# Moving two of the first four loads to ScalarE's queue in a fused retention and GELU kernel

## The chip, the cores and the metric

The kernel runs on one core of one Trainium2 chip. The metric is the device time of one execution in microseconds (us). Every ratio, with its 95% interval, is taken between the runs of two kernels of the same rounds; it is not quite the ratio of the medians that are quoted beside it. A difference counts as faster or slower from 2% on.

## The reference

Retention attention (8 batches, 8 heads, 576 positions, head size 64) feeds a two-layer network with a tanh GELU:

```python
scores = scale * np.matmul(q, k.transpose(0, 1, 3, 2))
gamma = 1.0 - 2.0 ** (-5.0 - np.arange(H, dtype=np.float32))
Dmat = np.where(rel >= 0, gamma[:, None, None] ** rel[None, :, :], 0.0)
ret = np.matmul(scores * Dmat[None], v)
# ... ret -> x, 4608 tokens x 512
h = x @ w_in                                    # 512 x 2048
g = 0.5 * h * (1.0 + np.tanh(c * (h + 0.044715 * h * h * h)))
out = g @ w_out                                 # 2048 x 512
```

## The kernel before

Work is laid out by hand in a plan of small steps. The plan fixes each engine's order. Only the start of the kernel ("the head", until the first long run of up-projection matmuls, called hp) matters for the main part of the change. Five pieces take part in it.

ScalarE's order begins with the decay factors. The trace shows a table load of 1.28 us in front of the first exp (at 0.73 us) and a second one, also of 1.28 us, in front of a dummy Gelu (at 3.99 us); the rest of the execution has none:

```python
nc.scalar.activation(out=p2[:, 3:4], in_=wz[:, 0:1], func=AF.Exp)      # first table load
# ...
for p in range(HP):
    nc.scalar.activation(out=gx[:, p], in_=gi, func=AF.Exp, bias=lg[:, 12:13], scale=lg[:, 8 + p : 9 + p])
nc.scalar.activation(out=sc, in_=ex, func=AF.Exp, bias=0.0, scale=-1.0)
gt = const.tile([128, HP], F32, name="gt")
nc.scalar.activation(out=gt, in_=lg[:, 8:12], func=AF.Exp, bias=0.0, scale=128.0)
nc.scalar.activation(out=p2[:, 3:4], in_=wz[:, 0:1], func=AF.Gelu_apprx_tanh)   # second table load
```

SP issues all loads of the head, each of 256 KB, in this order:

```python
load_qkv(0, 0, 0, "k", None)
load_qkv(0, 0, 0, "q", None)
load_qkv(0, 0, 1, "k", None)
load_qkv(0, 0, 0, "v", None)
load_qkv(0, 0, 1, "q", None)
# ... in load_qkv: nc.sync.dma_start(out=t..., in_=SRC[key][b, ...])
```

GpSimd (POOL) clears a buffer, then casts q and k. TensorE transposes the two cast tiles. The copies out of PSUM belong to ScalarE (the whole first tile and half of the second) and VectorE (the other half):

```python
(0, L(tbd_zero, 0, G)),
(0, L(cast_qk, 0, 0, 0, "q", G)),
(0, L(cast_qk, 0, 0, 0, "k", G)),
(0, L(mask)),
(0, L(tr, 0, 0, 0, 1, A)),      # ScalarE copies
(0, L(cast_v, 0, 0, 0, G)),
(0, L(tr, 0, 0, 0, 0, S2)),     # S2: half ScalarE, half VectorE
(0, L(score_mm, 0, 0, 0)),
```

Finally, `pads` puts a fixed number of dummy 128-column matmuls ("pads") in front of a step, for example `("tr", 0, 0, 1, 0): 24`.

## Time and profile before

| | before |
|---|---|
| time, median of the first 3 runs | 298.46 us (298.14 to 299.01) |
| span of the profiled run | 296.3 us |
| first copy on ScalarE starts | 5.78 us |
| VectorE's half copy starts | 6.80 us |
| first long hp run starts | 22.46 us |

The page's first part gives busy time, share of the span and instruction count of each engine. Its third part gives the DMA queues (packets, MB, share of the 16 DMA engines' time). Queue q1 is the one that SP feeds, q10 the one that ScalarE feeds (before the change, with stores at the end of the kernel only):

```profile
PE 288.9 (97%) x3748; PEld 208.6 (70%) x3748; DVE 230.7 (78%) x434; ACT 162.0 (55%) x316; POOL 122.4 (41%) x142
...
q1 hardware_dynamic: 94336, 51.26, 67.7%
q10 hardware_dynamic: 336, 0.66, 0.8%
```

TensorE is the bound, and ScalarE's average of 55% says nothing of the head, where it is full until 5.48 us. Two entries of TensorE's timeline (start, duration, engine, line, operation) serve as marks: the second group of score matmuls, and the long hp run.

```profile
10.41 0.42 PE L395 MATMUL st<-T 64*64 64x128 f16 x16
22.46 2.78 PE L669 MATMUL hp<-x,w_in_sb 128*128 128x256 f16 x24 [0.92 <-DVE x L535]
```

### The profile page before, as it was taken

What the parts mean: (1) busy time and instruction counts of PE and PEld (TensorE: products, weight loads), DVE (VectorE), ACT (ScalarE), POOL (GpSimd) and SP (SyncE); (2) the same over time, 40 slices, a digit from 0 to 9 for tenths busy, and PEclk for the clock granted to TensorE, in tenths of its full rate; (3) what the DMA queues carried; (4) which work ended last, traced back from release to release, by engine and by line L of the source; (5) the groups of instructions that cost most, each with busy time, mean ns of one, the idle gap of its engine ahead of it and who ended that gap; (6) DMA issues with size and microseconds to landing.
All of it is one profiled execution on the core that took longest, in us unless ns stands there. A gap on an engine that the chain in (4) does not pass through costs nothing.

```text
span 296.3 us, 8910 instructions
## 1 busy us (share of the span) xinstructions
PE 288.9 (97%) x3748; PEld 208.6 (70%) x3748; DVE 230.7 (78%) x434; ACT 162.0 (55%) x316; POOL 122.4 (41%) x142
## 2 busy tenths in 40 slices
PE   8989999999999999999999999999999999999995
PEld 6866578888884568656875587558755886786584
DVE  2795899999997795898569856877688198886753
ACT  7329789865546762665446544555345217605720
POOL 6734774476240144086026305469003005711760
PEclk9999999999999999999999999999999999999999
DMA  7999999868779999994998899482120003002204
GB/s 201 308 354 326 315 383 323 222 177 210 166 239 182 291 274 173 283 291 104 194 295 243 124 209 306 146 146 18 60 86 0 2 22 124 0 2 71 71 3 142
DMA packets 94712, 52.48 MB, mean 177 GB/s; under 512 B 38352, under 2 KB 88528, under 8 KB 94672
## 3 DMA queue, kind: packets, MB, share of 16 engines
q1 hardware_dynamic: 94336, 51.26, 67.7%
q10 hardware_dynamic: 336, 0.66, 0.8%
q8 instruction: 29, 0.48, 0.7%
q14 instruction: 11, 0.09, 0.1%
HBM read 36.70 MB, written 9.44 MB: 156 GB/s over the span
## 4 chain that ended last, share of the span: by engine, by line
PE 78%; DVE 13%; DMA 4%; ACT 2%; issue 1%; SPq 0%; POOL 0%; DVEq 0%; ACTq 0%
PE hp L583 31%; PE my L726 9%; PE mz L726 9%; PE mw L726 5%; PE mu L726 4%; PE mv L726 4%; PE hp L669 3%; DMA T<-kq 3%; DVE ret L408 3%; PE st L395 2%; PE xs L495 2%; PE py L613 2%; DVE ost L753 2%; PE xs L522 2%; DVE x L535 1%
## 5 line engine op out<-in xcount | busy, mean ns | idle before, releaser
L583 PE MATMUL hp<-x,w_in_sb 128*128 128x512 f16 x408 | 94.0, 379 | 0.0
L587 ACT ACTIVATE gT<-hp 128x512 f16<-128x512 f32 x112 | 65.8, 598 | 41.9 <-PE hp L583 40.1
L583 PEld LDWEIGHTS <-w_in_sb 128*128 128x128 f16 x448 | 42.5, 98 | 44.5 <-issue 0.3
L726 PEld LDWEIGHTS <-gT 128*128 128x128 f16 x576 | 55.8, 98 | 8.0
L232 POOL CAST kq<-ld 128x512 f16<-128x512 f32 x31 | 22.0, 716 | 57.7 <-DMA ld<-in_k_dram 42.3
L241 POOL TENSOR_TENSOR cv<-ld,sc 128x512 f16<-128x512 f32 x28 | 32.8, 1184 | 28.4 <-DMA ld<-in_v_dram 23.8
L408 DVE TENSOR_TENSOR ret<-st,cm 128x512 f16<-128x512 f32 x64 | 40.0, 681 | 4.2 <-PE st L395 3.9
L232 ACT CAST tbd<-ws 64x256 f16<-64x256 f32 x61 | 24.6, 403 | 22.5 <-DVE ws L476 21.9
L726 PE MATMUL my<-w_out_sb,gT 128*128 128x256 f16 x288 | 34.4, 273 | 0.0
L726 PE MATMUL mz<-w_out_sb,gT 128*128 128x256 f16 x288 | 34.4, 273 | 0.0
L726 PEld LDWEIGHTS <-gsum 128*128 128x128 f16 x288 | 28.0, 98 | 3.4
L698 DVE TENSOR_TENSOR gT<-gT 128x1024 f16<-128x1024 f16 x30 | 28.6, 960 | 0.2
L694 DVE TENSOR_TENSOR gsum<-gT 128x1024 f16<-128x1024 f16 x32 | 25.7, 802 | 2.7 <-ACT gT L656 2.7
L535 DVE TENSOR_TENSOR x<-xs,gx 128x512 f16<-128x512 f32 x32 | 21.5, 683 | 4.8 <-PE xs L522 4.6
L753 DVE TENSOR_TENSOR ost<-ost,mv 128x512 f32<-128x512 f32 x18 | 11.5, 683 | 16.6 <-issue 11.7
L686 DVE TENSOR_TENSOR gdia<-gT 128x512 f16<-128x512 f16 (+1 forms) x30 | 21.9, 731 | 2.8 <-ACT gT L587 2.1
L694 POOL TENSOR_TENSOR gsum<-gT 128x1024 f16<-128x1024 f16 x4 | 8.9, 2222 | 34.8 <-ACT gT L656 31.8
L669 PE MATMUL hp<-x,w_in_sb 128*128 128x256 f16 x160 | 19.0, 273 | 1.0 <-DVE x L535 0.9
L669 PEld LDWEIGHTS <-w_in_sb 128*128 128x128 f16 x160 | 15.3, 98 | 3.1 <-issue 1.3
L726 PE MATMUL mu<-w_out_sb,gsum 128*128 128x256 f16 x144 | 17.2, 273 | 0.1
L726 PE MATMUL mw<-w_out_sb,gdia 128*128 128x256 f16 x144 | 17.2, 273 | 0.0
L726 PE MATMUL mv<-w_out_sb,gsum 128*128 128x256 f16 x144 | 17.2, 273 | 0.0
(114 smaller groups left out, 402.2 us busy)
## 6 DMA issues: line engine op xcount, KB each, us to landing
ld<-in_k_dram SPq DMA_DIRECT2D x30, 256.0 KB, 5.3
ld<-in_q_dram SPq DMA_DIRECT2D x30, 256.0 KB, 5.4
ld<-in_v_dram SPq DMA_DIRECT2D x30, 256.0 KB, 5.7
out_dram<-ost SPq DMA_DIRECT2D x14, 512.0 KB, 5.2
loan<-in_moe_w_out_dram SPq DMA_DIRECT2D x12, 256.0 KB, 5.4
loan<-in_moe_w_in_dram SPq DMA_DIRECT2D x8, 256.0 KB, 5.8
ld<-in_moe_w_in_dram SPq DMA_DIRECT2D x8, 256.0 KB, 6.0
ld<-in_moe_w_out_dram SPq DMA_DIRECT2D x4, 256.0 KB, 5.6
```

The lines of the kernel that those rows point to most:

```text
L232: (eng.copy if eng is nc.scalar else eng.tensor_copy)(out=out, in_=in_)
L241: eng.tensor_tensor(out=unperm(att[b]["v"][:, s, hh, :]), in0=perm(t), in1=sc[:, 8 * hh : 8 * hh + 8] .rearrange("p (r h) -> p r h", r=2) ...
L408: nc.vector.tensor_tensor(out=x.rearrange("p (a m) -> p a m", a=2), in0=st[hl].rearrange("p (a m) -> p a m", a=2), in1=cm.rearrange("p r s ...
L535: nc.vector.tensor_tensor(out=xb[b][:, :, 2 * s + c].rearrange("p s q i -> p q s i"), in0=att[b]["x", s][c].rearrange("p (q s i) -> p q s ...
L583: nc.tensor.matmul(hp, w_in_sb[:, ct, 128 * f : 128 * f + 128], x[:, :, ct, :], start=(ct == 0), stop=(ct == 3),)
L587: nc.scalar.activation(out=self.g(f // 2)[:, f % 2], in_=hp, func=AF.Gelu_apprx_tanh)
L669: nc.tensor.matmul(hp[:, 256 * h : 256 * h + 256], w_in_sb[:, ct, 256 * j + 128 * h : 256 * j + 128 * h + 128], xb[self.b][:, :, 2 * u : 2 ...
L686: e.tensor_tensor(out=self.sa[:, j : j + n], in0=g[:, :, 0, 0:256], in1=g[:, :, 1, 256:512], op=ALU.add)
L694: e.tensor_tensor(out=self.sc[:, j : j + n], in0=g[:, :, 0], in1=g[:, :, 1], op=ALU.add)
L698: e.tensor_tensor(out=g.rearrange("p j h c -> p j (h c)")[:, :, 256:768].rearrange("p j (h c) -> p j h c", h=2), in0=g[:, :, :, 0:256], in ...
L726: nc.tensor.matmul(o, lhs(j, slice(128 * u, 128 * u + 128)), w_out_sb[:, j, w], start=((u == 0 or isinstance(t, list)) and j == 0 and not ...
L753: nc.vector.tensor_tensor(out=out, in0=in0, in1=t, op=op)
```

## The change

The intent is to get q, which the first cast waits for, and v sooner, by issuing them from a second queue at the same moment as SP issues k. ScalarE's exps move behind these two issues. The core of the diff:

```diff
-    nc.scalar.activation(out=p2[:, 3:4], in_=wz[:, 0:1], func=AF.Exp)
...
+    def exps():
+        nc.scalar.activation(out=p2[:, 3:4], in_=wz[:, 0:1], func=AF.Exp)
+        for p in range(HP):
+            nc.scalar.activation(out=gx[:, p], in_=gi, func=AF.Exp, ...)
+        ...                                    # sc, gt, dummy Gelu, as before
...
-            nc.sync.dma_start(
+            (nc.scalar if (b, key, s, hh) in AQ else nc.sync).dma_start(
...
+    AQ = {(0, "q", 0, 0), (0, "v", 0, 0)}
...
     load_qkv(0, 0, 0, "v", None)
+    exps()
     load_qkv(0, 0, 1, "q", None)
```

The rest of the diff touches the end of the kernel. The product called my runs its j loop outside. In the units with three PSUM banks, two subtractions of 256 columns become one of 512, ScalarE copies the first bank straight into the tile that they work on, and the two halves of that bank change places. Some helpers for half-sized state steps are defined but not called:

```diff
-            for m, k in ((2, 0), (1, 1)):
-                nc.vector.tensor_tensor(out=q4[:, m], in0=pw[:, 0:256], in1=c2[:, k], op=ALU.subtract)
+            nc.vector.tensor_tensor(
+                out=q[:, 1:3],
+                in0=pw[:, 0:256].unsqueeze(1).to_broadcast([128, 2, 256]),
+                in1=q[:, 1:3],
+                op=ALU.subtract,
+            )
...
+            order = [(u, j) for j in js for u in us] if m == "my" else [(u, j) for u in us for j in js]
```

More of the change, by code (lines that the diff above doesn't have):

```diff
@@ L119 @@
     gx = const.tile([128, HP, 2, 64], F32, name="gx")
-    for p in range(HP):
-        nc.scalar.activation(out=gx[:, p], in_=gi, func=AF.Exp, bias=lg[:, 12:13], scale=lg[:, 8 + p : 9 + p])
-    nc.scalar.activation(out=sc, in_=ex, func=AF.Exp, bias=0.0, scale=-1.0)
     gt = const.tile([128, HP], F32, name="gt")
-    nc.scalar.activation(out=gt, in_=lg[:, 8:12], func=AF.Exp, bias=0.0, scale=128.0)
-    nc.scalar.activation(out=p2[:, 3:4], in_=wz[:, 0:1], func=AF.Gelu_apprx_tanh)
+    def exps():
+        nc.scalar.activation(out=p2[:, 3:4], in_=wz[:, 0:1], func=AF.Exp)
+        for p in range(HP):
+            nc.scalar.activation(out=gx[:, p], in_=gi, func=AF.Exp, bias=lg[:, 12:13], scale=lg[:, 8 + p : 9 + p])
+        nc.scalar.activation(out=sc, in_=ex, func=AF.Exp, bias=0.0, scale=-1.0)
+        nc.scalar.activation(out=gt, in_=lg[:, 8:12], func=AF.Exp, bias=0.0, scale=128.0)
+        nc.scalar.activation(out=p2[:, 3:4], in_=wz[:, 0:1], func=AF.Gelu_apprx_tanh)
     tbd = [const.tile([128, NC, HP, 128], F16, name=f"tbd{i}") for i in range(2)]
@@ L442, in mask_tail, with state_h, state_mm @@
             a["rett", hl] = x
-    def state_mm(b, ss):
+    def state_h(b, s, hh):
+        state_mm(b, [s], (hh,))
+    def state_mm(b, ss, hhs=(0, 1)):
         a = att[b]
         us = [bank("us") for _ in range(2)]
-        pad(("us", b, ss[0]), us[0])
+        pad(("us", b, ss[0]) if len(hhs) == 2 else ("us", b, ss[0], hhs[0]), us[0])
         for n, s in enumerate(ss):
-            a["U", s] = us, n
-            for p in range(HP):
+            for hh in hhs:
+                a["U", s, hh] = us, n
+            for p in range(2 * hhs[0], 2 * hhs[-1] + 2):
                 hh, pp = divmod(p, 2)
@@ L464, in state_mm, with scan, scan_h, put @@
                             )
-    def scan(b, n):
+    def scan(b, n, hhs=(0, 1)):
         a = att[b]
         s, c = divmod(n, 2)
-        us, i = a["U", s]
-        uc = us[c][:, 256 * i : 256 * i + 256].rearrange("p (q d) -> p q d", d=64)
+        us, i = a["U", s, hhs[0]]
+        qs = slice(2 * hhs[0], 2 * hhs[-1] + 2)
+        nq = qs.stop - qs.start
+        uc = us[c][:, 256 * i : 256 * i + 256].rearrange("p (q d) -> p q d", d=64)[:, qs]
         if n > 0:
-            t = sb.tile([128, HP, 64], F32, tag="vs", name="vs", bufs=1)
-            nc.vector.tensor_tensor(out=t, in0=uc, in1=a["w", n - 1], op=ALU.add)
+            t = sb.tile([128, HP, 64], F32, tag="vs", name="vs", bufs=1)[:, qs]
+            nc.vector.tensor_tensor(out=t, in0=uc, in1=a["w", n - 1][:, qs], op=ALU.add)
             uc = t
-        w = sb.tile([128, HP, 64], F32, tag="ws", name="ws", bufs=2)
-        nc.vector.tensor_tensor(out=w, in0=uc, in1=gt.unsqueeze(2).to_broadcast([128, HP, 64]), op=ALU.mult)
-        a["w", n] = w
-    def put(b, n, eng):
+        if ("w", n) not in a:
+            a["w", n] = sb.tile([128, HP, 64], F32, tag="ws", name="ws", bufs=2)
+        nc.vector.tensor_tensor(
+            out=a["w", n][:, qs], in0=uc, in1=gt[:, qs].unsqueeze(2).to_broadcast([128, nq, 64]), op=ALU.mult
+        )
+    def scan_h(b, n, hh):
+        scan(b, n, (hh,))
+    def put(b, n, eng, hhs=(0, 1)):
         w = att[b]["w", n]
+        qs = slice(2 * hhs[0], 2 * hhs[-1] + 2)
         for hl in range(2):
             e = (A, V)[hl] if eng is S2 else eng
-            copy(e, tbd[b % 2][half[hl], n, :, half[hl]], w[half[hl]])
+            copy(e, tbd[b % 2][half[hl], n, qs, half[hl]], w[half[hl], qs])
+    def put_h(b, n, hh, eng):
+        put(b, n, eng, (hh,))
     def values(b, s):
@@ L518, in inter_mm @@
         if n > 0:
-            pad(("in", b, n), a["U", (n - 1) // 2][0][0])
+            pad(("in", b, n), a["U", (n - 1) // 2, 0][0][0])
             for p in range(HP):
@@ L620, in pair_a @@
             mm = self.pair_mm
-            mm(j, pv[:, 0:256], lambda c: f[:, 2 + c], lambda c: self.x_half(1, 2 + c), True)
-            mm(j, pv[:, 256:512], lambda c: f[:, 4 + c], lambda c: self.x_half(0, c))
+            mm(j, pv[:, 0:256], lambda c: f[:, 4 + c], lambda c: self.x_half(0, c), True)
+            mm(j, pv[:, 256:512], lambda c: f[:, 2 + c], lambda c: self.x_half(1, 2 + c))
             mm(j, pw[:, 0:256], lambda c: f[:, c], lambda c: self.xf[2][:, c], True)
@@ L628, in pair_q @@
             pv, pw, py = self.pair[j]
-            cp = sb.tile([128, 512], F32, tag="cv", name="cp", bufs=2)
-            q = sb.tile([128, 1024], F32, tag="T", name="q", bufs=4)
+            q = sb.tile([128, 4, 256], F32, tag="T", name="q", bufs=4)
             self.pair[j] = py, q
-            nc.scalar.copy(out=cp, in_=pv)
-            c2 = cp.rearrange("p (k c) -> p k c", k=2)
-            q4 = q.rearrange("p (m c) -> p m c", m=4)
+            nc.scalar.copy(out=q[:, 1:3], in_=pv.rearrange("p (k c) -> p k c", k=2))
             nc.vector.tensor_tensor(
-                out=q4[:, 0:4:3], in0=py.rearrange("p (k c) -> p k c", k=2), in1=c2, op=ALU.add
+                out=q[:, 0:4:3], in0=py.rearrange("p (k c) -> p k c", k=2), in1=q[:, 2:0:-1], op=ALU.add
             )
-            for m, k in ((2, 0), (1, 1)):
-                nc.vector.tensor_tensor(out=q4[:, m], in0=pw[:, 0:256], in1=c2[:, k], op=ALU.subtract)
+            nc.vector.tensor_tensor(
+                out=q[:, 1:3],
+                in0=pw[:, 0:256].unsqueeze(1).to_broadcast([128, 2, 256]),
+                in1=q[:, 1:3],
+                op=ALU.subtract,
+            )
         def pair_b(self, j):
@@ L648, in pair_s @@
             py, q = self.pair[j]
-            q4 = q.rearrange("p (m c) -> p m c", m=4)
             nc.vector.tensor_tensor(
-                out=q4[:, 1:3], in0=py.rearrange("p (k c) -> p k c", k=2), in1=q4[:, 1:3], op=ALU.add
+                out=q[:, 1:3], in0=py.rearrange("p (k c) -> p k c", k=2), in1=q[:, 1:3], op=ALU.add
             )
@@ L657, in pair_g @@
                 out=self.g(j).rearrange("p h (s c) -> p s h c", s=2),
-                in_=q.rearrange("p (s h c) -> p s h c", s=2, h=2),
+                in_=q.rearrange("p (s h) c -> p s h c", s=2),
                 func=AF.Gelu_apprx_tanh,
@@ L722, in product @@
             t = self.bank[m]
-            for u in us:
-                o = t[u] if isinstance(t, list) else t[:, 256 * u : 256 * u + 256]
-                for j in js:
-                    nc.tensor.matmul(
-                        o,
-                        lhs(j, slice(128 * u, 128 * u + 128)),
-                        w_out_sb[:, j, w],
-                        start=((u == 0 or isinstance(t, list)) and j == 0 and not more),
-                        stop=(j == NJ - 1), skip_group_check=True,
-                    )
+            order = [(u, j) for j in js for u in us] if m == "my" else [(u, j) for u in us for j in js]
+            for u, j in order:
+                nc.tensor.matmul(
+                    t[u] if isinstance(t, list) else t[:, 256 * u : 256 * u + 256],
+                    lhs(j, slice(128 * u, 128 * u + 128)),
+                    w_out_sb[:, j, w],
+                    start=((u == 0 or isinstance(t, list)) and j == 0 and not more),
+                    stop=(j == NJ - 1), skip_group_check=True,
+                )
         def quad(self, s, k):
@@ L795, in store_quad, with last @@
             )
-        def last(self):
-            for m in MS[:-1]:
+        def last(self, plan={}):
+            for i, m in enumerate(MS[:-1]):
                 self.down(m)
@@ L801, in last @@
                     self.store_quad(*q)
+                for step in plan.get(i, ()):
+                    step()
             for u in range(2):
```

## The prediction

> **What bounds the kernel now.** I read four views in this order: who waited for whom on TensorE, the busy time by stretch, the chain of work that ended last over the first 60 us, and the ordered timeline of each engine over the first 10 us.
>
> The wait view of TensorE (columns: engine and line, releaser, us in total, times, longest) says that over the whole kernel PE hardly waits for anything:
>
> ```profile
> PE hp L669 <- DVE x L535: 0.9, 1, 0.9
> PE st L395 <- DMA T<-kq: 0.7, 1, 0.7
> PE tr L342 <- ACT kq L232: 0.5, 1, 0.5
> PE tr L342 <- POOL kq L232: 0.2, 1, 0.2
> PE st L395 <- DVE T L232: 0.2, 1, 0.2
> ```
>
> The stretches (columns: stretch, PE busy, weight loads, DVE, ACT, POOL, granted clock, DMA share, GB/s) say where it is solid:
>
> ```profile
> 11.00:22.40 11.40, 9.84 (x238) 8.00 (x237) 10.42 (x22) 4.47 (x10) 6.67 (x12) 1.00 1.08 345
> 22.40:60.00 37.60, 37.31 (x467) 27.24 (x467) 32.82 (x64) 32.66 (x71) 20.69 (x23) 1.00 1.05 313
> 96.00:240.00 144.00, 144.00 (x1904) 97.89 (x1897) 109.45 (x196) 73.96 (x140) 50.41 (x60) 1.00 0.72 167
> 240.00:293.00 53.00, 52.89 (x407) 39.42 (x404) 40.16 (x64) 24.05 (x39) 22.39 (x10) 1.00 0.16 52
> ```
>
> From 22.46 us, where the first dense run of up-projection matmuls (hp) starts, to 292.9 us PE is the bound: 0.3 us idle up to 60, 0.8 us between 60 and 96 (0.7 of it the one wait for a transposing DMA), nothing after. Work there is fixed, so only the head, 0 to 22.46 us, can change the end. In the head PE counts as busy mostly because of padding matmuls on a zero tile (lines L147 and L149), which are fixed in number and keep their place in the order; so "busy" is no bound there, but the pads do hold back what stands behind them.
>
> The first useful work, from the timelines of SP, POOL, ACT and DVE (start us, duration us, engine, line, operation; in brackets the idle time before it and its releaser):
>
> ```profile
> 0.73 0.44 SPq L188 DMA_DIRECT2D ld<-in_k_dram  x1
> 1.23 0.49 SPq L188 DMA_DIRECT2D ld<-in_q_dram  x1
> ...
> 2.48 1.91 POOL L132 MEMSET tbd<- 128x512 f16 x4
> 4.68 1.17 POOL L232 CAST kq<-ld 128x512 f16<-128x512 f32 x2 [0.29 <-DMA ld<-in_q_dram]
> ...
> 0.73 1.28 ACT L88 ACT_TABLE_LOAD   x1 [0.73 <-PEq L1470]
> ...
> 3.99 1.28 ACT L125 ACT_TABLE_LOAD   x1
> 5.28 0.20 ACT L125 ACTIVATE p<-wz 128x1 f32<-128x1 f16 x1
> 5.78 0.99 ACT L232 COPY T<-tr 128x512 f16<-128x512 f16 x2 [0.29 <-PE tr L342]
> ...
> 6.80 0.29 DVE L232 COPY T<-tr 128x256 f16<-128x256 f16 x1 [3.81 <-ACT T L232]
> ```
>
> Three things are to be seen. The q load is what the first cast waits for, but only for 0.29 us: POOL is clearing tbd until 4.39 us anyway. ScalarE is busy from 0.73 to 5.48 us without a gap (table load, exps, table load), then idles only 0.29 us before it has to copy the first transposed tile. And VectorE, idle for 3.81 us, waits for ScalarE's copy: the two share the second tile, ScalarE first.
>
> [...] issues on SP stand about 0.5 us apart, while the first eight loads of 256 KB, once they flow, land about 0.9 us apart (completion times in the trace: 6.41, 7.34, 8.26, 9.14, 10.06, 10.90 us). [...] no trace of the kernel before shows two queues competing. [...] an issue occupies the issuing sequencer [...]. For ScalarE this is seen late in the same profile: four stores issued there take 1.79 us, 0.45 us each. [...] the trace shows 1.28 us for both, and the change keeps two loads.
>
> **The change, part by part.**
>
> (a) Loads. q(0,0,0) is issued on ScalarE at about 0.73 us instead of on SP at 1.23, and v(0,0,0) at about 1.2 instead of 2.32. The later SP loads move up by about one issue (0.5 us) or two (1.1 us). In the kernel before, k landed at 3.73 and q at 4.62 us. Sharing the engines from the start, the same 512 KB land together at about 3.9 to 4.1 us (an estimate: about 330 GB/s in the trace's half-microsecond slices from 2.5 us on). For the first cast this buys 4.68 - 4.39 = 0.29 us, no more, because then POOL's clearing ends last. On PE the eleven pads in front of the first transpose (4.37 us, 0.78 us long) end at 5.15 us, so of the 0.29 only 5.34 - 5.15 = 0.19 us arrive. v lands one to two us earlier and ends POOL's wait of 1.66 us at 7.51; but its product is used by state matmuls that the in-order PE reaches only at 10.63 us, so this lies beside the path.
>
> (b) ScalarE. Two issues go in front of everything: 2 x 0.44 to 0.49 us plus two gaps of 0.05 us, 0.95 to 1.05 us. All that follows in ScalarE's order has no gap to absorb it, so ScalarE comes free at 5.48 + 1.02 = 6.50 us. The first copy of a transposed tile then starts at 6.50 instead of 5.78: +0.72 us, although its input is 0.19 us earlier. The second (half) copy follows 0.5 us later, the pace of such copies back to back, at 7.00 instead of 6.40 us: +0.60 us (it used to wait for PE). VectorE's half follows: 7.40 instead of 6.80. The first score matmuls (st, 6.96 us before) need all of these, so they end 0.60 us later.
>
> (c) From there to 22.46 us. Behind the score matmuls PE has 24 pads, a transpose, 9 pads, a transpose (the chain from 7.50 to 9.91), then VectorE's copy, score matmuls, mask, scan and so on, and VectorE is busy 10.42 of 11.40 us in the next stretch. In this chain I find no wait for a load: the loads used here have landed 0.5 us or more before their turn. So nothing takes the 0.60 us back and it arrives whole at 22.46.
>
> (d) The rest of the diff. The product my now goes through j outside and the two halves inside; the same 16 matmuls of 0.11 us, and PE shows no wait in front of it that this could remove. In the three-bank units two subtractions of 0.413 us (the row of that form) become one of about 0.683 (the row of the addition of that shape), 6 times: 6 x 0.143 = 0.86 us of VectorE, in the stretch 240 to 293 where PE is 52.89 of 53.00 busy: beside the path. Half-sized state and scan steps are defined but not called. The comparison of instruction order shows nothing else moved.
>
> Sum: +0.60 us on 298.46 gives 299.06; I add a little for contention in the next paragraph and say 299.1 us.
>
> **Rivals.** *A: the gain arrives.* If issues on ScalarE cost its sequencer so little that the exps end by 5.7 us, the first copy starts at about 5.55 and the head is 0.2 us shorter: 298.2 us. For it: the change was presumably made because the load is the first wait in the chain. Against it: 1.79 us for four issues on this very queue. A gain beyond 0.3 us would need a wait that I don't see. *B: the issue is dearer.* [...] If ScalarE's issues stand behind SP's, they take up to 1.9 us instead of 1.0, and the loss grows from 0.6 to about 1.5 us: 300.0. For it: SP's own issues lengthen [...] (0.60 and then 1.52 us for the sixth and seventh). Against it: the first issues take 0.44 to 0.51 us while loads already flow. *C: the delay is absorbed later*, by the 0.9 us wait before the dense run or the 0.7 us wait for the transposing DMA at 95.8. For it: these are the only slack. Against it: both follow in chains from PE and VectorE work that moves by the same amount. Then about 298.5.
>
> **Range and chances.** Main line 299.06, A 298.2, B 300.0, C 298.5; the kernel before varies over 0.9 us (298.14 to 299.01). An interval of 298.2 to 300.1 us holds all of them. The 2% limits lie at 292.5 and 304.4 us, which none of these reaches: within 2% 0.98, faster 0.01, slower 0.01.
>
> **What would show it.** Right: the first table load at about 1.75 us; q landing by about 4.1 and the first cast at about 4.4; the first copy on ScalarE at about 6.5 with no idle time, or a short one, before it; VectorE's half copy at about 7.4; the first dense hp run at about 23.1 instead of 22.46, and the same length from there to the end. Wrong: a first table load before 1.2 us; a first copy before 5.8; a dense run that starts before 22.46 (then some load did bound the head), or a time after 22.46 that differs by more than 0.3 us (then my, the three-bank units or the transposing DMA matter).

The sum came to +0.60 us on 298.46, 299.06 us, and the step to 299.1 is the guess for contention, with no trace behind it. That q and k share the DMA engines from the start, in (a), was the assumption; for rival B nothing was shown beyond SP's two long issues (0.60 and 1.52 us). The 1.28 us "for both" are the two table loads of ScalarE.

## The result, and the profile after

| | before | after |
|---|---|---|
| time, median of 4 runs | 298.30 us (297.93 to 299.01) | 299.18 us (298.47 to 299.31) |
| ratio | 1 | 1.0022 (0.9997 to 1.0047): within 2% |
| span of the profiled run | 296.3 us | 297.4 us |

The same two parts of the page for the changed kernel:

```profile
PE 289.3 (97%) x3748; PEld 209.0 (70%) x3748; DVE 232.1 (78%) x428; ACT 162.1 (55%) x316; POOL 123.2 (41%) x142
...
q1 hardware_dynamic: 93280, 50.74, 63.6%
q10 hardware_dynamic: 1392, 1.18, 1.5%
```

The two loads are now in ScalarE's queue: q10 went from 336 to 1392 packets, and q1 lost the same 1056. Nothing else in these totals explains a microsecond. VectorE lost six instructions (12 subtractions became 6).

The changed kernel's timeline over the first 12 us, with the groups that answer to those of the prediction (start, duration, engine, line, operation; in brackets the idle time before it and what ended it):

```profile
0.73 0.51 ACTq L190 DMA_DIRECT2D ld<-in_q_dram  x1
0.73 0.99 SPq L190 DMA_DIRECT2D ld<-in_k_dram  x2
...
1.27 0.56 ACTq L190 DMA_DIRECT2D ld<-in_v_dram  x1
...
1.86 1.28 ACT L122 ACT_TABLE_LOAD   x1 [1.86 <-issue]
...
4.90 1.17 POOL L234 CAST kq<-ld 128x512 f16<-128x512 f32 x2 [0.51 <-DMA ld<-in_q_dram]
...
5.12 1.28 ACT L127 ACT_TABLE_LOAD   x1
...
6.52 0.84 ACT L234 COPY T<-tr 128x512 f16<-128x512 f16 x2
...
7.39 0.29 DVE L234 COPY T<-tr 128x256 f16<-128x256 f16 x1 [4.40 <-ACT T L234]
...
11.01 0.42 PE L397 MATMUL st<-T 64*64 64x128 f16 x16
```

Read it from the left. ScalarE spends 0.51 and 0.56 us on the two issues, and its first table load starts at 1.86 us, 1.13 later than before. The exps and the second table load follow without a gap. The first copy starts at 6.52 us with no bracket behind it: it no longer waits for TensorE; ScalarE itself is late. The chain view, followed back from 60 us, says the same: its first pieces are ScalarE's two issues, the two table loads with the exps between them, and then this copy. VectorE's half copy then moves from 6.80 to 7.39 us, and the score matmuls from 10.41 to 11.01. The first cast meanwhile is not earlier. It moved from 4.68 to 4.90 us and still waits for q, now for 0.51 us.

Where q's gain went is seen in the DMA view of the changed kernel, between 1.5 and 2.5 us and then between 2.5 and 4.5 us (columns as above):

```profile
q1 hardware_dynamic: 160, 0.08, 29.4%
q10 hardware_dynamic: 2, 0.00, 0.3%
```

```profile
q1 hardware_dynamic: 725, 0.36, 63.2%
q10 hardware_dynamic: 536, 0.27, 45.4%
```

Both queues got their first issue at 0.73 us, but in the first of these stretches SP's queue moved 160 packets and ScalarE's 2. From 2.5 us on ScalarE's queue had to share the engines with SP's two k loads. By the completion times in the trace k landed at 4.40 us instead of 3.75, and q at 4.85 instead of 4.62. (Some of these times stand 0.02 us lower in the recorded texts; nothing hangs on it.)

After the head, the long hp run, and TensorE's waits of the changed kernel (engine and line, releaser, us in total, times, longest):

```profile
22.94 2.78 PE L686 MATMUL hp<-x,w_in_sb 128*128 128x256 f16 x24 [0.81 <-DVE x L552]
```

```profile
PE hp L686 <- DVE x L552: 1.3, 2, 0.8
...
PE st L397 <- ACT tbd L234: 0.4, 1, 0.4
```

And the stretch from 60 to 96 us, first of the kernel before, then of the changed kernel, whose stretch from 22.4 to 60 us is shown too (columns: stretch, PE busy, weight loads, DVE, ACT, POOL, granted clock, DMA share, GB/s):

```profile
60.00:96.00 36.00, 35.21 (x599) 27.95 (x601) 33.18 (x70) 20.58 (x45) 15.66 (x18) 1.00 0.83 192
```

```profile
22.40:60.00 37.60, 36.06 (x455) 26.06 (x455) 33.07 (x60) 30.85 (x68) 20.82 (x23) 1.00 0.98 305
60.00:96.00 36.00, 35.67 (x597) 28.91 (x596) 33.85 (x71) 20.46 (x44) 15.66 (x18) 1.00 0.83 208
```

The hp run starts 0.48 us later, not 0.60. Between 22.4 and 60 us TensorE did 37.31 - 36.06 = 1.25 us less work than before. Of this 0.48 is the later start, which leaves 0.77 us more idle time than before (1.00 us against 0.23). Most of the 1.00 us is two waits: one of 0.44 us at 43.78 for ScalarE's cast of the state (the "st <- ACT tbd" line) and one of 0.45 us at 51.00 for VectorE's x (the second of the two "hp <- DVE x" waits). Between 60 and 96 us it did 0.46 us more, because the wait for the transposing DMA that the kernel before shows is not there. The balance, 1.25 - 0.46 = 0.79 us, with another 0.16 us lost between 96 and 240 us, accounts for 0.95 of the 1.1 us between the two spans. This is the account of two single executions; the experiments show how far the part after the hp run differs from one execution to the next.

### The profile page after: what moved, and what is told of

Read it like the earlier page. It is cut to its first block, busy times and chain, and to the rows that moved or that the text cites. A ratio compares the mean times of both kernels' runs of the same rounds, so it can differ in the third digit from the quotient of the medians. Undisturbed runs are those within 1.5% of the kernel's fastest.

```text
span 297.4 us, 8903 instructions
## 1 busy us (share of the span) xinstructions
PE 289.3 (97%) x3748; PEld 209.0 (70%) x3748; DVE 232.1 (78%) x428; ACT 162.1 (55%) x316; POOL 123.2 (41%) x142
## 3 DMA queue, kind: packets, MB, share of 16 engines
q10 hardware_dynamic: 1392, 1.18, 1.5%
## 4 chain that ended last, share of the span: by engine, by line
PE 80%; ACT 7%; DMA 5%; DVE 5%; issue 2%; ACTq 0%; SPq 0%; DVEq 0%
PE hp L600 28%; PE my L742 10%; PE mz L742 10%; PE mu L742 5%; PE mw L742 5%; PE mv L742 5%; PE hp L686 3%; DMA loan<-in_moe_w_out_dram 2%; PE xs L512 2%; PE st L397 2%; ACT gT L604 2%; DMA ld<-in_moe_w_out_dram 2%; PE py L630 2%; PE xs L539 2%; ACT tbd L234 1%
## 5 line engine op out<-in xcount | busy, mean ns | idle before, releaser
L234 POOL CAST kq<-ld 128x512 f16<-128x512 f32 x31 | 23.9, 778 | 57.9 <-DMA ld<-in_k_dram 42.9
L243 POOL TENSOR_TENSOR cv<-ld,sc 128x512 f16<-128x512 f32 x28 | 31.4, 1134 | 27.3 <-DMA ld<-in_v_dram 22.8
```

Source lines behind the costliest of these rows:

```text
L234: (eng.copy if eng is nc.scalar else eng.tensor_copy)(out=out, in_=in_)
L243: eng.tensor_tensor(out=unperm(att[b]["v"][:, s, hh, :]), in0=perm(t), in1=sc[:, 8 * hh : 8 * hh + 8] .rearrange("p (r h) -> p r h", r=2) ...
```

## The experiments

The theory: ScalarE's own time spent issuing delays its first copy, and this is all that matters. Rivals: the rest of the diff costs the time; or the loads do, by their new order or by sharing the engines. A second question grew from the profile: is the 0.77 us of later idle time part of the change, or chance?

The first four runs shared 11 runs of the kernel before (median 298.12 us), the next four another 11 (297.99), the last three another 11 (297.73, with a wide spread from 296.65 to 300.89). All kernels computed correct results. This table gathers the marks of each profile (start times in us) and the times:

| kernel | first table load | first copy, ScalarE | half copy, VectorE | long hp run | time, median (range) | ratio (95%) |
|---|---|---|---|---|---|---|
| before | 0.73 | 5.78 | 6.80 | 22.46 | 298.30 | 1 |
| after | 1.86 | 6.52 | 7.39 | 22.94 | 299.18 (298.47–299.31) | 1.0022 (0.9997–1.0047) |
| r1_rest | 0.73 | 6.20 | 7.22 | 22.66 | 297.82 (297.30–298.84) | 0.9995 (0.9977–1.0013) |
| r2_loads | 1.87 | 6.53 | 7.58 | 23.58 | 299.25 (298.25–301.06) | 1.0040 (1.0015–1.0065) |
| r3_delay | 0.73 | 6.54 | 7.41 | 23.18 | 299.00 (298.27–299.77) | 1.0032 (1.0015–1.0049) |
| r4_gelu | 1.86 | 6.01 | 7.03 | 22.93 | 298.38 (298.05–300.36) | 1.0023 (0.9999–1.0046) |
| r5_qfirst | 0.73 | 5.44 | 6.46 | 22.32 | 297.73 (297.09–299.55) | 0.9996 (0.9969–1.0023) |
| r6_one | 1.25 | 6.28 | 7.51 | 23.49 | 298.81 (297.93–300.43) | 1.0025 (0.9999–1.0050) |
| r7_pads | 0.73 | 5.75 | 6.76 | 22.16 | 298.52 (297.70–301.95) | 1.0030 (0.9991–1.0068) |
| r8_both | 0.73 | 6.29 | 7.30 | 22.48 | 297.57 (297.26–297.96) | 0.9981 (0.9963–0.9998) |
| r9_again | 1.87 | 6.53 | 7.41 | 23.20 | 298.98 (298.38–299.99) | 1.0036 (0.9998–1.0074) |
| r10_vlate | 1.86 | 6.52 | 7.40 | 22.94 | 298.59 (298.43–300.04) | 1.0032 (0.9990–1.0073) |
| r11_both | 0.73 | 6.29 | 7.55 | 23.10 | 298.58 (297.65–298.87) | 1.0012 (0.9975–1.0049) |

The marks come from one profiled execution of each kernel, the times from four to six. A profiled execution can lie at the edge of its kernel's range: in r1, r4, r5, r7 and r10 it was the fastest of the six. From the start of the long hp run to the end of the span the thirteen profiles took between 272.84 (r1) and 274.46 us (the changed kernel; the kernel before took 273.84). This spread is larger than the whole effect, so a mark in the head tells what happened in the head, and only the timed runs tell what it was worth.

Three intervals leave out "no difference": those of r2 and r3 (slower) and of r8 (faster, and not repeated, as will be seen). The two of the changed kernel itself just include it.

### r1_rest: everything but the two loads

The changed kernel with both loads back on SP:

```diff
-    AQ = {(0, "q", 0, 0), (0, "v", 0, 0)}
+    AQ = set()
```

> The changed kernel with all four first loads back on SP; the other parts of the diff (order of the matmuls of my, three-bank units with one subtraction) stay. Theory (ScalarE set free late is the loss): ScalarE's first copy at 5.78 us, dense hp run at 22.46 us as before, time within 0.15% of the kernel before. Rival (the reordered my or the three-bank units cost time): the head is as before, but the span is still about 1 us longer than before, time up 0.2 to 0.35%.

The ratio is 0.9995 (0.9977 to 1.0013). The rest of the diff costs nothing that this can show, and that rival falls. In the profile the first copy is nevertheless 0.42 us later than in the kernel before, and the timeline says why:

```profile
4.44 1.38 PE L149 MATMUL tr<-ident,wz 128*128 128x128 f16 x11
...
6.20 0.99 ACT L234 COPY T<-tr 128x512 f16<-128x512 f16 x2 [0.72 <-PE tr L344]
```

ScalarE was ready at its old time and idled 0.72 us, waiting for a transpose. The eleven pads in front of that transpose took 1.38 us, where they took 0.78 in the kernel before. The change has no hand in these pads; they turn up again below.

### r2_loads: the two loads alone

The kernel before, with only the parts of the diff shown first under "The change" (the `exps` function, the choice of queue, `AQ`).

> The kernel before with only the two loads on ScalarE's queue and the exps behind them. Theory: the whole difference is here: first table load at 1.86 us, first copy at 6.52, dense hp run at 22.94, time up 0.2 to 0.35% as in the changed kernel. Rival (other parts of the diff): as the kernel before, within 0.1%.

The ratio is 1.0040 (1.0015 to 1.0065): the loss is here, in the two loads and the later exps together. Its size in the profile was larger than in the changed kernel, with the hp run at 23.58 us. Part of that is the slow pads again (1.38 us). Part is a collision that the timeline of r2 shows between VectorE and GpSimd:

```profile
9.54 1.25 DVE L234 CAST kq<-ld 128x512 f16<-128x512 f32 x1
```

```profile
9.46 1.04 POOL L243 TENSOR_TENSOR cv<-ld,sc 128x512 f16<-128x512 f32 x1 [1.58 <-DMA ld<-in_v_dram]
```

VectorE's cast takes 0.42 us in the kernel before. Here it starts 0.08 us after GpSimd's product of v and ends 0.29 us after it, taking 1.25 us. Why is not shown, but the pair has a pattern: in the first 11 us of the thirteen profiles eight VectorE casts of this form are slowed (0.46 to 1.25 us); each began while a product of v ran on GpSimd, and each ended 0.28 to 0.30 us after it. In the changed kernel VectorE came first, by 0.09 us, and it was GpSimd's product that grew, by 0.20 us, less than the 0.33 us that the cast still had to run:

```profile
9.35 0.42 DVE L234 CAST kq<-ld 128x512 f16<-128x512 f32 x1
...
9.44 1.24 POOL L243 TENSOR_TENSOR cv<-ld,sc 128x512 f16<-128x512 f32 x1 [1.57 <-DMA ld<-in_v_dram]
```

So the change brings these two operations within 0.1 us of each other, and small differences decide who pays: in r2 and r6, whose pads were slow, GpSimd came first. In the kernel before they are far apart: the cast starts at 8.76 us, the product at 10.15.

### r3_delay: the delay without any load moved

The kernel before, with three superfluous exps, about the time of the two issues:

```diff
-    for p in range(HP):
+    for p in (0, 1, 2, 0, 1, 2, 3):
```

> The kernel before, all loads on SP, with three more exps of 128x128 on ScalarE in the head (they write the same values again), about 1.16 us. Theory: ScalarE's first copy at about 6.65 to 6.8 us instead of 5.78, VectorE's half copy at about 7.55 instead of 6.80, dense hp run 0.6 to 0.75 us later than 22.46, with no load moved; time up 0.2 to 0.4%. Rival (the loads' landing is what matters): dense hp run within 0.1 us of 22.46, no change in time.

The timeline of r3, with no load moved, has the marks of the changed kernel:

```profile
6.54 0.84 ACT L232 COPY T<-tr 128x512 f16<-128x512 f16 x2
...
7.41 0.29 DVE L232 COPY T<-tr 128x256 f16<-128x256 f16 x1 [4.41 <-ACT T L232]
...
23.18 2.78 PE L669 MATMUL hp<-x,w_in_sb 128*128 128x256 f16 x24 [0.92 <-DVE x L535]
```

The ratio is 1.0032 (1.0015 to 1.0049) and the profiled span 297.4 us, that of the changed kernel. ScalarE's second table load came 1.14 us later than before (5.13 instead of 3.99), and this delay alone gives a loss of the size of the change's. This is the strongest evidence for the theory, because it moves no load. It shows that the delay is enough, not that the loads add nothing: the intervals of r2 and r3 leave room for that. The hp mark is weaker evidence than the ratio: the eleven pads were slow here too (1.38 us, hidden behind ScalarE), and VectorE's next cast took 0.98 us instead of 0.42.

### r4_gelu: taking the delay back

The changed kernel, with the dummy Gelu (and so the second table load of 1.28 us) moved behind the first copies:

```diff
+    def gelu_table():
         nc.scalar.activation(out=p2[:, 3:4], in_=wz[:, 0:1], func=AF.Gelu_apprx_tanh)
...
         (0, L(tr, 0, 0, 0, 0, S2)),
+        (0, L(gelu_table)),
         (0, L(score_mm, 0, 0, 0)),
```

> The changed kernel with the dummy gelu, and so the second table load, placed behind ScalarE's first two copies, where it has 2.45 us of idle time. Theory: ScalarE is through its exps at about 5.1 us, so its first copy starts when PE's transpose ends, at about 6.0 us (q lands at 4.83 us, later than before): 0.22 us later than before instead of 0.74; dense hp run about 0.2 us later than 22.46 instead of 0.48. Rival (the loads' landing, or ScalarE's issues themselves): the first copy or the dense run stays at 6.5 or 22.9 us.

The first half came: the copy started at 6.01 us and waited for TensorE again, as it does when ScalarE is not the bound.

```profile
6.01 0.99 ACT L236 COPY T<-tr 128x512 f16<-128x512 f16 x2 [0.91 <-PE tr L346]
7.01 1.28 ACT L129 ACT_TABLE_LOAD   x1
```

The second half did not: the hp run started at 22.93 us, as late as in the changed kernel. VectorE's half copy was 0.23 us later than before (q's late landing remains), and further on a cast of w_in on VectorE took 0.87 us instead of 0.42, beside casts of the same kind on GpSimd. The ratio, 1.0023, lies between "no loss" and the changed kernel's, and its interval holds both. This run is inconclusive on the time. It does show a second cost beneath the first: with ScalarE out of the way the chain view starts with the q load, which landed at 4.85 us as in the changed kernel, and 0.23 us remain at the copy. Even with ScalarE on time, then, the moved q load would not have been a gain.

### r5_qfirst: what an earlier q is worth

The kernel before, with q loaded ahead of k:

```diff
-    load_qkv(0, 0, 0, "k", None)
     load_qkv(0, 0, 0, "q", None)
+    load_qkv(0, 0, 0, "k", None)
```

> The kernel before with its first two loads exchanged on SP (q, then k), nothing on ScalarE. Asks what an earlier q is worth where ScalarE is not held up. Theory (the earlier q can gain only what POOL's clearing and the pads leave, 0.19 us): q lands at about 3.7 us, first cast at 4.42 us, first transpose at about 5.15 us, ScalarE's first copy at about 5.6, VectorE's half copy at about 6.6; dense hp run at about 22.25 us if the pads run at full pace; time 0 to 0.1% less. Rival (the landing of q is the real bound of the head): first copy and dense run move up by 0.5 us or more, time 0.2% less.

This gives q the head start that the change meant to give, without a cost:

```profile
4.35 1.16 POOL L232 CAST kq<-ld 128x512 f16<-128x512 f32 x2
5.44 0.99 ACT L232 COPY T<-tr 128x512 f16<-128x512 f16 x2
```

The cast starts when GpSimd is free, with no wait for a load. ScalarE's copy comes 0.34 us earlier, and has no wait either: the transpose ends at 5.41 us, and ScalarE is free at nearly the same moment, its second table load and dummy Gelu having just ended. At the hp run 0.14 us was left (22.32 against 22.46), and the ratio is 0.9996 (0.9969 to 1.0023). A perfect load of q is worth a tenth or two, which the time cannot resolve.

### r6_one: only q on ScalarE

As r2, with `AQ = {(0, "q", 0, 0)}`.

> The kernel before with q alone on ScalarE's queue and the exps behind it. Theory (each issue on ScalarE pushes its exps back by about 0.55 us, of which 0.29 us were idle): first table load at about 1.32 us, first copy at about 6.0, VectorE's half copy at about 6.9 instead of 6.80 and 7.39; dense hp run 0.1 to 0.2 us later than before, about a quarter of the change's loss; time 0 to 0.15% more. Rival (a second queue by itself costs, or is worth, the whole difference): first copy at 6.5 or later, time as in the changed kernel; or a first copy before 5.78 and a gain.

ScalarE's one issue took 0.48 us, and its table loads ran 0.52 us later than before, so that it was ready for its copy again before the transpose was. Still the hp run came at 23.49 us, far more than the half of the delay explains. Both disturbances of r2 were there: pads of 1.38 us, and the same cast on VectorE at 1.23 us beside GpSimd's product, which had started 0.10 us earlier. So this run does not give the price of one issue. It does show that the profile of one execution carries disturbances as large as the effect. Like r4 it also has a ratio of the size of the changed kernel's (1.0025, 0.9999 to 1.0050) although ScalarE was not what held the first copy.

### r7_pads: is the head's length worth its face value?

The kernel before, with five pads fewer in front of a transpose in the head:

```diff
-        ("tr", 0, 0, 1, 0): 24,
+        ("tr", 0, 0, 1, 0): 19,
```

> The kernel before with 19 instead of 24 pads in front of the third transpose of the head. Theory (in the head the in-order PE's pads, not loads, hold back what follows; VectorE has cast the fourth tile by 9.18 us while PE comes to it at 9.5): 5 pads of 0.056 us, 0.28 us, are gained up to the dense hp run, at about 22.2 us; time 0.05 to 0.1% less. Rival (something else holds the fourth transpose): dense run at 22.46, no change.

The hp run came 0.30 us earlier, at 22.16 us. The time did not follow: 298.52 us, ratio 1.0030 with the interval from 0.9991 to 1.0068. The profiled execution was the fastest of six, and one of the six took 301.95 us. The result on the time is unclear, and fewer pads are not a gain.

### r8_both and r11_both: a version that might beat both

The changed kernel with `AQ = set()`, q loaded before k, and 19 pads.

> The changed kernel with all loads on SP, q before k, and 19 pads: an attempt at a version that beats both. Theory: 0.19 us from the earlier q and 0.28 us from the pads, dense hp run at about 22.0 us; time 0.1 to 0.2% less than the kernel before. Rival: the two gains are the same slack, 0.28 us at most.

The ratio of 0.9981 (0.9963 to 0.9998) looked like a small gain, although in its profile the pads were slow (1.38 us) and the hp run no earlier than before. It was repeated:

> The version of r8_both again, beside the changed kernel in the same rounds. Theory: 0.1 to 0.2% less than the kernel before, 0.3 to 0.6% less than the changed kernel. Rival (its gain was chance): within 0.05% of the kernel before.

The second ratio is 1.0012 (0.9975 to 1.0049), with the pads slow again. The gain was not repeated. In this profile the hp run started at 23.10 us, as late as in the delayed kernels, with no load moved and ScalarE waiting 0.80 us for the transpose: slow pads and a slow cast (0.79 us) can do that by themselves. No version that beats both kernels is established.

### r9_again and r10_vlate: the collision

The changed kernel once more, unchanged, and the changed kernel with two SP loads exchanged, so that the v half that GpSimd multiplies lands later and this collision should not occur:

```diff
-    load_qkv(0, 0, 1, "v", None)
     load_qkv(0, 1, 1, "k", None)
+    load_qkv(0, 0, 1, "v", None)
```

> The changed kernel itself once more, for a ratio of the same rounds as the next two. Theory (a fixed loss of about 0.5 us in the head, and on top of it a coin flip: VectorE's cast of the q tile at about 9.3 us against GpSimd's cv operation at 9.44): ratio 1.002 to 1.004, spread wider than that of the kernel before; where GpSimd comes first, the cast takes 1.2 us instead of 0.42. Rival (the first measurement was chance): ratio within 0.1% of 1.

> The changed kernel with the load of v(0,0,1) exchanged with the one after it, so that GpSimd's cv operation that waits for it starts about 0.9 us later, at about 10.3 us. Theory of the collision: VectorE's cast of q at 9.3 to 9.6 us takes 0.42 us whatever the pace of the pads, and only the delay of ScalarE is left: dense hp run 0.4 to 0.6 us later than before with pads at full pace (up to 0.9 with slow ones), time 0.1 to 0.25% more than before and with less spread than the changed kernel. Rival (the collision is no part of the loss): time as r9_again.

In r9 the pair stood again within a hair, VectorE first by 0.01 us; GpSimd's product grew to 1.30 us. In r10 they were apart (the product at 10.31 us, at its normal 1.04). The hp run starts at 23.20 and 22.94 us, but the times agree: 298.98 and 298.59, ratios 1.0036 and 1.0032 against the same runs of the kernel before. How much the collision adds in the timed runs stays open. r10's ratio is hardly smaller without it; and in r3 GpSimd's product began 0.25 us after the cast and grew to 1.06 us only, though there another cast of VectorE, at 7.62 us, took 0.98 us beside GpSimd's first product. In these profiles a delayed VectorE met GpSimd at one place or another.

r9 also gives a second measure of the change itself. Together with the first (1.0022), and with r2 (1.0040), the loss is put at 0.2 to 0.4%: 0.7 to 1.2 us. These are the middles of wide intervals.

Now the second question, the 0.77 us of later idle time. The same stretch of r9, the same kernel:

```profile
22.40:60.00 37.60, 36.39 (x460) 26.51 (x459) 32.18 (x62) 31.51 (x69) 20.58 (x23) 1.00 1.00 303
```

TensorE did 37.31 - 36.39 = 0.92 us less work than before, and the hp run came 0.74 us later, so only 0.18 us is new idle time. By the same sum r2 has none (36.23 us of work, hp run 1.12 us later), and r3 has 0.35. Most of the 0.77 us was thus one execution's, and no run shows that any of it belongs to the change.

## Why the prediction was right or wrong

The predicted time was 299.1 us (298.2 to 300.1); 299.18 was measured, within 2% as expected. Its steps:

- **(a) The loads: wrong.** The step assumed that both queues share "the same 512 KB" from the start, so that q and k land together at 3.9 to 4.1 us. The second queue moved almost nothing between 1.5 and 2.5 us (2 packets against 160 of SP's queue), and then shared with two k loads (536 packets against 725 up to 4.5 us). q landed at 4.85 us, later than before, and the first cast started at 4.90, not 4.4. The predicted 0.19 us of gain on TensorE was a loss of 0.23 at the first transpose (5.57 instead of 5.34 us). This did no harm to the sum, because step (b) had ScalarE as the bound from there on, with or without the gain. The limit that the step named, GpSimd's clearing, was right: in r5 q came early and the cast began at 4.35 us, when GpSimd was free.
- **(b) ScalarE: the mechanism right; the hundredths are luck.** Predicted were a table load at 1.75, the copy at 6.50 and the half copy at 7.40 us; measured were 1.86, 6.52 and 7.39. The score matmuls came 0.60 us later, the very figure. The issues were dearer than thought (0.51 and 0.56 instead of 0.44 to 0.49 us): they delayed ScalarE by 1.13 us, not 1.02. The step also took ScalarE to be free at 5.48 us, where the dummy Gelu's record ends; but the copy that follows such a Gelu starts 0.11 us after the Gelu's start (6.52 after 6.41), so ScalarE was ready at about 5.39 (an estimate from these two numbers). The two errors of a tenth cancel. The mechanism itself is seen in the changed kernel's chain, and r3 shows the same marks without a moved load.
- **(c) "It arrives whole at 22.46": half right.** In the changed kernel's profile 0.48 of 0.60 us arrived. On the way a cast of w_in cost 0.11 us more (0.53 instead of 0.42), and two casts of the state on VectorE took 0.59 us together instead of 0.81. In r9, the same kernel, it was 0.74, and in r3 0.72. The sentence "the same length after" was wrong in its profile: TensorE idled 0.77 us more between 22.4 and 60 us. It was then repaid by 0.46 between 60 and 96. The prediction named a time after 22.46 that differs by more than 0.3 us as a sign that it was wrong, and pointed to my, the three-bank units or the transposing DMA; in this pair of profiles it differs by 0.62 us (274.46 instead of 273.84). r1 clears my and the three-bank units, and the other profiles, r9 above all, show that such differences come without the change. The two errors cancel in part, which is why the time fits so well; a difference of 0.1 us between prediction and result is luck at this spread.
- **(d) The rest of the diff: right.** r1 shows a ratio of 0.9995. The merged subtraction takes 0.691 us (predicted 0.683) for two of 0.413, beside the path.

The rivals: A, the gain arrives, is refuted by the table load at 1.86 us and by q's landing at 4.85. B, issues that stand behind SP's, is refuted by 0.51 and 0.56 us. C expected the delay to be absorbed in one of two waits. The wait before the hp run only shrank from 0.92 to 0.81 us. The wait of 0.70 us for the transposing DMA did vanish, and the profile alone would suggest that it took up the delay. But it is absent from all twelve other profiles, among them r1, r5 and r7, where ScalarE is not delayed. So it belongs to one execution of the kernel before rather than to the change; that it was chance is argued from these profiles, and the timed runs could not show it.

What remains open is the exact size of the loss (0.7 to 1.2 us against 0.6 by the sum) and how the surplus splits between the collision of VectorE and GpSimd and other disturbances. Open too is whether the moved loads add to the loss: no run moves them with ScalarE wholly on time, and r4 and r6, which come nearest, have ratios of 1.0023 and 1.0025. That the delay of ScalarE is all that matters is therefore not shown; that it is enough is shown by r3, which, like r2, was run once and against the same runs of the kernel before.

## What to carry to other kernels

An issue moved to another engine is work put in front of that engine's own (here 0.51 and 0.56 us on ScalarE): count its time against the slack of that engine until its first consumer, here about 0.4 us of slack (0.29 us of it recorded as idle time) against 1.13 us of delay. Before hastening a load, look at what else holds its consumer (here GpSimd's clearing until 4.39 us); the order of the loads on one queue brought q sooner at no cost, and even that left only 0.14 us at the hp run. And where single profiles differ by half a microsecond from execution to execution, follow one mark through several of them before explaining a difference in the last few tenths.

## What else the traces show

- In the changed kernel an issue on ScalarE took 0.51 and 0.56 us, while loads of 256 KB landed about 0.9 us apart (at 7.36, 8.28, 9.17 and 10.09 us in the kernel before), and a delay of about two such issues on ScalarE alone (1.14 us in r3) costs 0.3%. The issues that SP no longer makes had taken 0.49 and 0.51 us there: what one sequencer was spared, the other took on.
- Two queues given their first issue at the same 0.73 us moved their first packets at 1.83 us (SP) and 2.43 us (ScalarE), and q landed at 4.85 us instead of 4.62 although its issue started 0.5 us earlier. Why ScalarE's queue started later is open.
- Each table load took 1.28 us, and no further cost is to be seen around the second one of the changed kernel: it starts at 5.12 us, 0.02 us after the last exp, and the next activation at 6.41, 0.01 us after it.
- The same eleven pads took 0.78 us in six profiles, 0.86 in r7 and 1.38 in the other six. The profile's granted clock does not show it: over the first 11 us it reads 1.00 in r1 (slow pads) and in the kernel before alike, so the durations of known small matmuls have to be read instead. What slows the pads is not shown.
